# A layer of state-space scan and gated MLP on one core: three projections of a chunk gathered in one phase of full-row matmuls

## The chip, the cores and the metric

The kernel runs on 1 core of one Trainium2 chip. The metric is the time of one execution on the device, in microseconds (us); lower is better. A core has five engines that work side by side, each through its own queue in order: TensorE (PE: matrix products, with its weight loads shown as PEld), VectorE (DVE), ScalarE (ACT), GpSimd (POOL) and SyncE (SP), which here issues transfers (DMAs). Data lie in SBUF, sums of matrix products in PSUM banks.

## What is computed

The input x has 2048 rows of 448 values, in bfloat16. The rows are normalised; the result feeds a state-space recurrence (part A) and a gated MLP (part B), and both are multiplied and added to the input:

```python
def _A_ref(x, Lambda_re, Lambda_im, B_re, B_im, C_re, C_im, log_dt, Dskip):
    dt = jnp.exp(log_dt)
    Lam_bar = jnp.exp(dt * Lam)
    B_bar = ((Lam_bar - 1.0) / Lam)[:, None] * Bmat
    Bu = jnp.einsum("bld,pd->blp", x + 0j, B_bar)
    for t in range(L):
        h = Lam_bar[None, :] * h + Bu[:, t, :]
    y = 2.0 * jnp.einsum("blp,dp->bld", hseq, Cmat).real + x * Dskip[None, None, :]
def _B_ref(x, w_gate, w_up, w_down):      # w_gate, w_up: 448 x 1792; w_down: 1792 x 448
    h = _sigmoid(x @ w_gate) * (x @ w_up)
    return h @ w_down
xn = _layernorm(x)
return x + _A_ref(xn, ...) * silu(_B_ref(xn, ...))
```

## The kernel before, in words

The 2048 rows are cut into four chunks (c = 0 to 3) of 512. `xnT` holds a chunk's normalised rows transposed. Per chunk there are these kinds of work:

- **Gate and up steps** (`gu_step`, `gu_mm` at L709 and L710): 14 steps a chunk, seven blocks `m` for each of gate and up. Each step is seven pairs of matmuls with 64 contraction rows; the two of a pair run at the same time in the two halves of the array. A step fills one of three PSUM slots `gu` (two banks each). `gu_evac` reads it out: a gate step by ScalarE (L723, tanh), an up step by VectorE (L726, times the up values, into `hF`). In chunk 0 the seven gate steps come first, then the seven up steps; in the others they alternate.
- **Input projections of the scan** (`b_units`): four units `pt` a chunk, the products with the input matrix `bT`. Units 0 to 2 have 512 columns in each of two banks; unit 3 is narrow, 256 columns in each, with its weights in `bT6`. The 448 values of a row are three times 128 and one rest of 64. So each unit has a pair of 64-row matmuls (L762 and L763, for unit 3 L765 and L767) and six 128-row ones (L777, for unit 3 L780). ScalarE copies the sums to `bus` (L788; for unit 3 three copies, L792, L794, L796).
- **The scan** (`ssm_pair`, `ssm_stack`, called by `whole`): VectorE products with sine and cosine tables, two scans along the rows, two products more, and the state sequence `hT`. POOL prepares the coefficients, ScalarE and VectorE the tables (`tables`, L577 to L602).
- **Down** (`down`, L892): 14 full-row matmuls for each of four 128-row blocks `j`, into one of two PSUM banks `acc`, then ScalarE's silu (L898, `g_t`).
- **Skip products** (`yout`, L917): seven full-row matmuls from `hT` into `acc`, then three VectorE operations (L923, L925, L927: add, multiply, add) and the store.

Down of chunk c - 1 and the skip products of chunk c - 2 run while chunk c is in its gate and up steps. In each chunk there are two places where full-row work stands between 64-row steps: `b_units(c, (0, 1), ...)` and `b_units(c, (2, 3), ...)`. In each, the 64-row pairs of two units go first, with `start=True`, then a down (the `mid` argument), then the units' full-row matmuls, then a skip product, a down and a skip product (chunks 2 and 3). Between the two places stand three gate and up steps.

The order of PE's queue is that of the calls. For the other engines a planner (`Plan`) decides: each piece of work is registered with an assumed cost, what it reads and what it writes, and the planner places pieces by the latest time at which PE's fixed order needs them. So a change of PE's order also moves work on VectorE, ScalarE and POOL. `SW` is the cost that the planner assumes for a change between 64-row and full-row matmuls. Each engine then works strictly in that order.

Of the kernel before, what the change touches and what calls it, by code (L numbers as in the profile page):

```python
# [14 lines left out]
ACT = mybir.ActivationFunctionType  # L15
# [5 lines left out]
P = 128  # L21
# [41 lines left out]
def act(n, ap=0):  # L63
    return 0.05 + 0.000833 * n + 0.093 * ap
# [9 lines left out]
class Plan:  # L74
# [10 lines left out]
    def add(self, eng, cost, fn, r=(), w=(), dma=0, lat=None, chain=False, name="", rate=230e3):  # L85
        o = Op()
        o.idx, o.eng, o.cost, o.fn, o.dma, o.name = len(self.ops), eng, cost, fn, dma, name
        o.lat = LAT.get(eng, 0.0) if lat is None else lat
        o.pre, o.suc, o.rate = {}, [], rate
        o.slot = None  # L90
        if dma and eng != "POOL":
            o.slot, self.n_dma = self.n_dma, self.n_dma + 1
        o.start = o.end = None
        for k in r:
            if k in self.w:
                self._edge(self.w[k], o, True)
        for k in w:
            for q in self.r.get(k, ()):
                self._edge(q, o, False)
            if k in self.w:  # L100
                self._edge(self.w[k], o, True)
        for k in w:
            self.w[k] = o
            self.r[k] = []
        for k in r:
            if k not in w:
                self.r.setdefault(k, []).append(o)
        if chain or eng == "PE" or (eng == "DVE" and self.seq):
            key = ("chain", eng)
            if key in self.last_of:  # L110
                self._edge(self.last_of[key], o, None)
            self.last_of[key] = o
        self.ops.append(o)
        return o
# [131 lines left out]
def kernel(  # L246
# [274 lines left out]
    def xr(c, lo=0, hi=TPC):  # L521
        return [("xnT", c % 3, j, h) for j in range(lo, hi) for h in "ab"]
# [171 lines left out]
    def next_gu():  # L694
        a = gu_n[0] % 3
        gu_n[0] += 1
        return a
# [51 lines left out]

    bus_n = [0]  # L750

    def b_units(c, pts, mid=None):
        x = xnT[c % 3]
        slots = [next_gu() for _ in pts]
        bk = [("bT", 0), ("bT", 1), ("bT3", 0), ("bT3", 1), "bT3l"] + (
            [("bT6", 0), ("bT6", 1)] + [("bT6", i, h) for i in range(2) for h in range(2)] if 3 in pts else [])

        def pairs():
            for pt, a in zip(pts, slots):
                if pt < 3:  # L760
                    ps = slice(pt * P, pt * P + P)
                    T.matmul(gu[a][:, 0, :], lhsT=bT[0:H, 3, 0, ps], rhs=x[0:H, 6, :], start=True, stop=False)  # L762
                    T.matmul(gu[a][:, 1, :], lhsT=bT[H:P, 3, 1, ps], rhs=x[H:P, 5, :], start=True, stop=False)  # L763
                else:
                    T.matmul(gu[a][:, 0, 0:256], lhsT=bT6[0:H, 3, :], rhs=x[0:H, 6, 0:256],  # L765
                             start=True, stop=False)
                    T.matmul(gu[a][:, 1, 0:256], lhsT=bT6[H:P, 3, :], rhs=x[H:P, 5, 256:512],  # L767
                             start=True, stop=False)
        add("PE", 0.216 * len(pts), pairs, r=xr(c) + bk, w=[("gu", a) for a in slots], name=f"bp{c}.{pts[0]}")
        if mid:  # L770
            mid()
        for n, (pt, a) in enumerate(zip(pts, slots)):
            def fulls(pt=pt, a=a):
                for i in range(2):
                    for kt in range(3):
                        if pt < 3:
                            T.matmul(gu[a][:, i, :], lhsT=bT[:, kt, i, pt * P:pt * P + P], rhs=x[:, 2 * kt, :],  # L777
                                     start=False, stop=(kt == 2))
                        else:
                            T.matmul(gu[a][:, i, 0:256], lhsT=bT6[:, kt, :],  # L780
                                     rhs=x[:, 2 * kt, i * 256:i * 256 + 256], start=False, stop=(kt == 2))
            add("PE", (6 * 0.215 if pt < 3 else 6 * 0.11) + (0 if n or mid else SW), fulls,
                r=xr(c) + bk + [("gu", a)], w=[("gu", a)], name=f"b{c}.{pt}")
            u = bus_n[0] % NBUS
            bus_n[0] += 1
            bus_of[c, pt] = u
            if pt < 3:
                add("ACT", act(1024), lambda u=u, a=a: A.copy(out=bus[u][:], in_=gu[a][:]),  # L788
                    r=[("gu", a)], w=[("bus", u)])
            else:  # L790
                h2 = lambda t: t.rearrange("p (i n) -> p i n", i=2)
                add("ACT", act(512), lambda u=u, a=a: A.copy(out=h2(bus[u][:, 0, :]), in_=gu[a][:, :, 0:256]),  # L792
                    r=[("gu", a)], w=[("bus", u)])
                add("ACT", 0.6, lambda u=u, a=a: A.copy(out=h2(bus[u][0:H, 1, :]), in_=gu[a][H:P, :, 0:256]),  # L794
                    r=[("gu", a)], w=[("bus", u, 1)])
                add("ACT", 0.6, lambda u=u, a=a: A.copy(out=h2(bus[u][H:P, 1, :]), in_=gu[a][0:H, :, 0:256]),  # L796
                    r=[("gu", a)], w=[("bus", u, 2)])

    bus_of = {}

# [50 lines left out]
    def ssm_stack(c):  # L851
        pt = 3
        u = bus_of[c, pt]
        ia, ta = nxt("ta")
        iz, z = nxt("z")
        iw, wv = nxt("wv")
        tk = [("cos", 3), ("sin", 3)]
        dve(dve2(1024), lambda: V.tensor_tensor(out=ta[:], in0=bus[u][:], in1=cs3[:], op=ALU.mult),
            [("bus", u), ("bus", u, 1), ("bus", u, 2)] + tk, [("ta", ia)])
        dve(dve2(512), lambda: V.tensor_tensor(out=z[:, 0, :], in0=ta[:, 0, :], in1=ta[:, 1, :], op=ALU.add),  # L860
            [("ta", ia)], [("z", iz)])
        rb = C("r")[:, pt:pt + 1].to_broadcast((P, L))
        dve(1.194, lambda: V.tensor_tensor_scan(out=wv[:, 0, :], data0=rb, data1=z[:, 0, :],
                                                initial=(st[pt][:, 0, :] if c else 0.0), op0=ALU.mult, op1=ALU.add),
            ["r", ("z", iz)] + ([("st", pt)] if c else []), [("wv", iw)])
        for h in range(2):
            o, i = slice(h * H, h * H + H), slice((1 - h) * H, (1 - h) * H + H)
            add("ACT", 0.6, lambda o=o, i=i: A.copy(out=wv[o, 1, :], in_=wv[i, 0, :]), r=[("wv", iw)], w=[("wv", iw, 1 + h)])
        wk = [("wv", iw), ("wv", iw, 1), ("wv", iw, 2)]
        if c < NC_ - 1:  # L870
            dve(0.12, lambda: V.tensor_tensor(out=tqs[pt][:, 0, :], in0=wv[:, 1, L - 1:L], in1=sinL[:, 3, 0, :], op=ALU.mult),
                wk + ["sinL"], [("tq", pt)])
            dve(0.12, lambda: V.scalar_tensor_tensor(out=st[pt][:, 0, :], in0=wv[:, 0, L - 1:L], scalar=cosL[:, pt, :],
                                                    in1=tqs[pt][:, 0, :], op0=ALU.mult, op1=ALU.subtract),
                wk + ["cosL", ("tq", pt)], [("st", pt)])
        ia, tcx = nxt("ta")
        dve(dve2(1024), lambda: V.tensor_tensor(out=tcx[:], in0=wv[:], in1=cs3[:], op=ALU.mult), wk + tk, [("ta", ia)])
        dve(dve2(512), lambda: V.tensor_tensor(out=hT[c % 2][:, 6, :], in0=tcx[:, 0, :], in1=tcx[:, 1, :], op=ALU.subtract),
            [("ta", ia)], hkeys(c, pt))
# [113 lines left out]
        gu_step(0, i)  # L993
    stats_for(2)
    stats_for(3)
    b_units(0, (0, 1))
    b_units(0, (2, 3))
    for i in range(13, 14):
        gu_step(0, i, i == 13)
    c_scale()  # L1000
    whole(0)

    halves(1, ((0, "g"), (1, "g")))
    one(1, 0, "u")
    prepare(2)
    b_units(1, (0, 1), lambda: down(0, 0, True))
    down(0, 1)
    for i in range(3, 6):
        gu_step(1, i, i == 3)
    b_units(1, (2, 3), lambda: down(0, 2, True))  # L1010
    down(0, 3)
    for i in range(6, 14):
        gu_step(1, i, i == 6)
    whole(1)
    for c in (2, 3):
        for i in range(0, 4):
            gu_step(c, i)
        b_units(c, (0, 1), lambda: down(c - 1, 0, True))
        yout(c - 2, 0)
        down(c - 1, 1)  # L1020
        yout(c - 2, 1)
        for i in range(4, 7):
            gu_step(c, i, i == 4)
        b_units(c, (2, 3), lambda: down(c - 1, 2, True))
        yout(c - 2, 2)
        down(c - 1, 3)
        yout(c - 2, 3)
        if c == 2:
            prepare(3)
        for i in range(7, 14):  # L1030
            gu_step(c, i, i == 7)
        whole(c)

    yout(2, 0, True)
# [53 lines left out]
```

## Time and profile before

| | us |
|---|---|
| median of 4 runs | 187.07 (186.75 to 188.67) |
| the profiled execution | 186.84 |
| its span, first to last instruction | 185.0 |
| VectorE busy | 165.9 |
| ScalarE busy | 93.0 |

The span is the time from the first instruction to the last in the profile; the execution's own time is 1.84 us longer. Busy time of an engine is the union of its instructions. In a timeline each row gives start, duration, engine, source line, operation, tiles written and read with their shapes, the number of merged instructions, and in brackets the idle time before it with what released it. Matmuls are pipelined, so their durations overlap: what counts is the distance from one start to the next. In a row by windows, the width of the window comes first, then busy time (and number of instructions) of PE, PEld, DVE, ACT and POOL, then the granted clock of TensorE, and the DMAs' share and rate.

Two rows of the costliest groups give the scale; after the bar stand busy time in us and the mean ns of one:

```profile
L892 PE MATMUL acc<-wd,hF 128*128 128x448 bf16 x168 | 33.8, 353 | 0.0
L777 PE MATMUL gu<-xnT,bT 128*128 128x512 bf16 x72 | 16.9, 379 | 0.0
```

### The profile page before, as it was taken

To read this page: it belongs to the slowest core of one execution; us is meant where nothing else is said; L and a number is where in the kernel's file an instruction comes from. 1 tells how busy PE (TensorE), PEld (TensorE's weight loads), DVE (VectorE), ACT (ScalarE), POOL (GpSimd) and SP (SyncE) were. 2 spreads that over 40 slices of the span, in tenths; PEclk is the share of its full clock that TensorE was granted. 3 is DMA by queue.
4 is the path that set the end of the run, shared out by engine and by line. 5 is a ranking of instruction groups with operands and counts; after the bars stand their busy time and mean duration, and the time that the engine had idled before them with its cause. 6 is when DMAs were issued, how large, how long until landed. Compare 5 with 4: busy or idle time off the path is not lost.

```text
span 185.0 us, 3527 instructions
## 1 busy us (share of the span) xinstructions
PE 179.3 (97%) x1375; PEld 88.2 (48%) x1375; DVE 165.9 (90%) x295; ACT 93.0 (50%) x140; POOL 38.4 (21%) x93
## 2 busy tenths in 40 slices
PE   7999999999999999999999999999999999999991
PEld 2684443564445444444445444444445544455550
DVE  3833999999999899999999999899999999999763
ACT  3549996973999994225465432327124526211110
POOL 7134452930268926000012100000000000000000
PEclk9999999999999999999999999999999999999999
DMA  5999999499202330000023200000000000002120
GB/s 135 275 217 233 220 217 136 81 265 208 88 4 50 78 74 0 0 0 4 0 57 84 61 26 0 4 25 25 0 25 4 25 25 4 25 0 76 51 78 25
DMA packets 30257, 13.43 MB, mean 73 GB/s; under 512 B 19744, under 2 KB 30240, under 8 KB 30240
## 3 DMA queue, kind: packets, MB, share of 16 engines
q1 hardware_dynamic: 28336, 12.05, 30.3%
q10 hardware_dynamic: 1808, 1.15, 2.4%
q8 instruction: 11, 0.18, 0.4%
q14 instruction: 6, 0.05, 0.1%
q0 software_dynamic: 96, 0.00, 0.0%
HBM read 6.77 MB, written 1.84 MB: 47 GB/s over the span
## 4 chain that ended last, share of the span: by engine, by line
PE 80%; DVE 11%; ACT 4%; issue 1%; DMA 1%; DVEq 0%
PE gu L709 39%; PE acc L892 15%; PE acc L917 11%; PE gu L892 6%; PE gu L777 5%; DVE hF L726 2%; DVE wv L831 2%; DMA x_all<-in_A_x_dram 1%; ACT ctmp L675 1%; DVE ta L824 1%; PE gu L780 1%; PE acc L502 1%; ACT bus L788 1%; DVE tb L825 1%; PE gu L710 1%
## 5 line engine op out<-in xcount | busy, mean ns | idle before, releaser
L709 PE MATMUL gu<-xnT,wG 64*128 64x512 bf16 (+1 forms) x231 | 46.1, 344 | 0.3 <-DVE xnT L510 0.3
L710 PE MATMUL gu<-xnT,wG 64*128 64x512 bf16 (+1 forms) x231 | 46.1, 344 | 0.0
L709 PE MATMUL gu<-xnT,wU 64*128 64x512 bf16 x196 | 46.0, 376 | 0.0
L710 PE MATMUL gu<-xnT,wU 64*128 64x512 bf16 x196 | 46.0, 376 | 0.0
L723 ACT ACTIVATE sig<-gu 128x1024 f32<-128x1024 f32 x21 | 21.4, 1022 | 30.3 <-PE gu L710 27.9
L892 PE MATMUL acc<-wd,hF 128*128 128x448 bf16 x168 | 33.8, 353 | 0.0
L892 PEld LDWEIGHTS <-hF 128*128 128x128 bf16 x224 | 21.4, 98 | 21.1 <-issue 1.7
L709 PEld LDWEIGHTS <-wG 64*128 64x128 bf16 x231 | 21.3, 94 | 20.9 <-issue 1.9
L709 PEld LDWEIGHTS <-wU 64*128 64x128 bf16 x196 | 18.1, 94 | 23.4 <-issue 1.3
L726 DVE SCALAR_TENSOR_TENSOR hF<-sig,gu 128x1024 bf16<-128x1024 f32 x21 | 25.4, 1211 | 1.9 <-PE gu L710 1.6
L831 DVE TENSOR_TENSOR_SCAN wv<-c_r,st,z 128x512 bf16<-128x512 f32 x18 | 22.9, 1274 | 0.0
L917 PE MATMUL acc<-cT,hT 128*128 128x448 bf16 (+1 forms) x112 | 22.4, 344 | 0.0
L710 PEld LDWEIGHTS <-wG 64*128 64x128 bf16 x231 | 21.3, 94 | 0.0
L710 PEld LDWEIGHTS <-wU 64*128 64x128 bf16 x196 | 18.1, 94 | 0.0
L777 PE MATMUL gu<-xnT,bT 128*128 128x512 bf16 x72 | 16.9, 379 | 0.0
L917 PEld LDWEIGHTS <-hT 128*128 128x128 bf16 x119 | 11.3, 98 | 10.0 <-issue 0.4
L898 ACT ACTIVATE g_t<-acc 128x448 bf16<-128x448 f32 x12 | 6.5, 540 | 16.1 <-PE acc L892 13.0
L425 DVE BATCH_NORM_STATS2 bst<-x_all 128x6 f32<-128x448 bf16 x12 | 7.0, 611 | 7.1 <-DMA x_all<-in_A_x_dram 7.1
L788 ACT CAST bus<-gu 128x1024 bf16<-128x1024 f32 x12 | 12.0, 1005 | 2.3 <-PE gu L777 2.3
L478 POOL COPY xn<-xn 128x64 bf16<-128x64 bf16 x12 | 5.8, 481 | 29.3 <-ACT xn L475 29.1
L923 DVE TENSOR_TENSOR o_t<-acc,xd 128x448 bf16<-128x448 f32 (+1 forms) x16 | 9.5, 594 | 2.6 <-PE acc L917 2.4
L898 ACT ACTIVATE g_t<-gu 128x448 bf16<-128x448 f32 x4 | 2.2, 544 | 18.8 <-PE gu L892 18.8
(142 smaller groups left out, 260.5 us busy)
## 6 DMA issues: line engine op xcount, KB each, us to landing
out_dram<-o_t SPq DMA_DIRECT2D x15, 112.0 KB, 1.7
wd<-in_B_w_down_dram SPq DMA_DIRECT2D x2, 784.0 KB, 5.0
x_all<-in_A_x_dram SPq DMA_DIRECT2D x3, 448.0 KB, 5.0
wU<-in_B_w_up_dram SPq DMA_DIRECT2D x2, 448.0 KB, 11.1
wU<-in_B_w_up_dram SPq DMA_DIRECT2D x2, 336.0 KB, 7.2
wG<-in_B_w_gate_dram SPq DMA_DIRECT2D x2, 224.0 KB, 5.7
wG<-in_B_w_gate_dram ACTq DMA_DIRECT2D x2, 224.0 KB, 6.4
xnT<-xn SPq DMA_TRANSPOSE x24, 2.4
```

What stands on the lines that cost most here:

```text
L425: add("DVE", 0.6, lambda: V.bn_stats(out=bst[b][:], in_=x_all[:, t, :]), r=[("x", t)], w=[("bst", b)])
L709: T.matmul(gu[a][:, 0, ts], lhsT=w_[0:H, s, ms], rhs=x[0:H, s, ts], start=(s == 0), stop=(s == 6))
L710: T.matmul(gu[a][:, 1, ts], lhsT=w_[H:P, (s + 1) % 7, ms], rhs=x[H:P, s, ts], start=(s == 0), stop=(s == 6))
L723: add("ACT", act(1024), lambda: A.activation(th, gu[a][:], ACT.Tanh, scale=0.5), r=[("gu", a)], w=[tk])
L726: add("DVE", dve1(1024), lambda: V.scalar_tensor_tensor(out=ho, in0=th, scalar=1.0, in1=gu[a][:], op0=ALU.add, op1=ALU.mult), r=[("gu", a) ...
L777: T.matmul(gu[a][:, i, :], lhsT=bT[:, kt, i, pt * P:pt * P + P], rhs=x[:, 2 * kt, :], start=False, stop=(kt == 2))
L788: add("ACT", act(1024), lambda u=u, a=a: A.copy(out=bus[u][:], in_=gu[a][:]), r=[("gu", a)], w=[("bus", u)])
L831: dve(1.194, lambda k=k: V.tensor_tensor_scan(out=wv[:, k, :], data0=rb, data1=z[:, k, :], initial=(st[pt][:, k, :] if c else 0.0), op0=AL ...
L892: T.matmul(d, lhsT=hF[c % 2][:, m, h, js], rhs=wd[:, ft, :], start=(ft == 0), stop=(ft == FT - 1))
L898: add("ACT", act(448), lambda: A.activation(g_t[g][:], d, ACT.Silu, scale=0.5), r=[key, "silutab"], w=[("gt", g)])
L917: T.matmul(y, lhsT=hT[c % 2][:, hm, js], rhs=cT[:, cm, c0:c1], start=(i == 0), stop=(i == 6))
L923: add("DVE", dve1(n), lambda od=od, y=y, c0=c0, c1=c1: V.tensor_tensor(out=od, in0=y, in1=xq[:, c0:c1], op=ALU.add), r=[key, ("xd", q)], w ...
```

## The change

There is one full-row phase a chunk in place of two. `b_phase` puts the 64-row pairs of units 3, 0 and 1 first, then their full-row matmuls, then (`mid`) all four downs of chunk c - 1 with the four skip products of chunk c - 2 between them, then unit 2: its full-row matmuls open the sum and its 64-row pair closes it, directly ahead of the next 64-row step. Unit 3 moves from a `gu` slot into the two `acc` banks, 256 columns in each, and its sums are copied by six ScalarE instructions of 256 columns in place of three of 512. Chunk 0's last up step now stands ahead of the phase. The number and the sizes of the matmuls stay the same.

```diff
-    def b_units(c, pts, mid=None):
+    def b_phase(c, mid=None):
         x = xnT[c % 3]
-        slots = [next_gu() for _ in pts]
...
+        slots = [next_gu() for _ in range(3)]
+        a3 = (next_acc(), next_acc())
...
+        rs = [(slice(0, H), 6), (slice(H, P), 5)]
+
+        def halfrows(pt, start):
+            for i, (hs, s_) in enumerate(rs):
+                if pt < 3:
+                    T.matmul(gu[slots[pt]][:, i, :], lhsT=bT[hs, 3, i, pt * P:pt * P + P], rhs=x[hs, s_, :],
+                             start=start, stop=not start)
+                else:
+                    T.matmul(acc[a3[i]][:, 0:256], lhsT=bT6[hs, 3, :], rhs=x[hs, s_, i * 256:i * 256 + 256],
+                             start=start, stop=not start)
 
         def pairs():
...
+            for pt in (3, 0, 1):
+                halfrows(pt, True)
+
+        def fulls(pt, first):
+            for i in range(2):
+                for kt in range(3):
+                    if pt < 3:
+                        T.matmul(gu[slots[pt]][:, i, :], lhsT=bT[:, kt, i, pt * P:pt * P + P], rhs=x[:, 2 * kt, :],
+                                 start=(first and kt == 0), stop=(not first and kt == 2))
+                    else:
+                        T.matmul(acc[a3[i]][:, 0:256], lhsT=bT6[:, kt, :],
+                                 rhs=x[:, 2 * kt, i * 256:i * 256 + 256], start=False, stop=(kt == 2))
...
+            if pt < 3:
+                add("ACT", act(1024), lambda: A.copy(out=bus[u][:], in_=gu[slots[pt]][:]), r=key(pt), w=[("bus", u)])
+                return
+            for i in range(2):
+                ns = slice(i * 256, i * 256 + 256)
+                for h, (d, q, l) in enumerate(((slice(0, P), slice(0, P), 0), (slice(0, H), slice(H, P), 1),
+                                               (slice(H, P), slice(0, H), 1))):
+                    add("ACT", 0.3, lambda ns=ns, d=d, q=q, l=l, i=i: A.copy(out=bus[u][d, l, ns], in_=acc[a3[i]][q, 0:256]),
...
+        add("PE", 0.54, pairs, r=xr(c) + bk + bk6, w=key(3) + key(0) + key(1), name=f"bp{c}")
+        for pt in (3, 0, 1):
+            add("PE", (1.29 if pt < 3 else 0.66) + (SW if pt == 3 else 0), lambda pt=pt: fulls(pt, False),
+                r=xr(c) + bk + bk6 + key(pt), w=key(pt), name=f"b{c}.{pt}")
+            evac(pt)
+        if mid:
+            mid()
+        add("PE", 1.29, lambda: fulls(2, True), r=xr(c) + bk, w=key(2), name=f"b{c}.2")
+        add("PE", 0.22 + SW, lambda: halfrows(2, False), r=xr(c) + bk + key(2), w=key(2), name=f"bp{c}.2")
+        evac(2)
...
-    b_units(0, (0, 1))
-    b_units(0, (2, 3))
-    for i in range(13, 14):
-        gu_step(0, i, i == 13)
+    gu_step(0, 13)
+    b_phase(0)
...
-    b_units(1, (0, 1), lambda: down(0, 0, True))
-    down(0, 1)
-    for i in range(3, 6):
-        gu_step(1, i, i == 3)
-    b_units(1, (2, 3), lambda: down(0, 2, True))
-    down(0, 3)
-    for i in range(6, 14):
-        gu_step(1, i, i == 6)
+    b_phase(1, lambda: [down(0, j) for j in range(4)])
+    for i in range(3, 14):
+        gu_step(1, i)
     whole(1)
     for c in (2, 3):
+        def mid(c=c):
+            for j in range(4):
+                down(c - 1, j)
+                yout(c - 2, j)
         for i in range(0, 4):
             gu_step(c, i)
...
+        b_phase(c, mid)
         if c == 2:
             prepare(3)
-        for i in range(7, 14):
-            gu_step(c, i, i == 7)
+        for i in range(4, 14):
+            gu_step(c, i)
         whole(c)
```

More of the change, by code (lines that the diff above doesn't have):

```diff
@@ L750 @@
     bus_n = [0]
-    def b_units(c, pts, mid=None):
+    def b_phase(c, mid=None):
         x = xnT[c % 3]
-        slots = [next_gu() for _ in pts]
-        bk = [("bT", 0), ("bT", 1), ("bT3", 0), ("bT3", 1), "bT3l"] + (
-            [("bT6", 0), ("bT6", 1)] + [("bT6", i, h) for i in range(2) for h in range(2)] if 3 in pts else [])
-        def pairs():
[L759 to L783, printed above, removed]
@@ new lines, in b_phase @@
+        slots = [next_gu() for _ in range(3)]
+        a3 = (next_acc(), next_acc())
+        bk = [("bT", 0), ("bT", 1), ("bT3", 0), ("bT3", 1), "bT3l"]
+        bk6 = [("bT6", 0), ("bT6", 1)] + [("bT6", i, h) for i in range(2) for h in range(2)]
+        rs = [(slice(0, H), 6), (slice(H, P), 5)]
[7 more added lines that the diff above has]
+                             start=start, stop=not start)
@@ L784, in b_units, with key, evac @@
+        def key(pt):
+            return [("gu", slots[pt])] if pt < 3 else [("acc", a) for a in a3]
+        def evac(pt):
             u = bus_n[0] % NBUS
@@ L787, in b_units @@
             if pt < 3:
[L788 to L797, printed above, removed]
+                add("ACT", act(1024), lambda: A.copy(out=bus[u][:], in_=gu[slots[pt]][:]), r=key(pt), w=[("bus", u)])
[5 more added lines that the diff above has]
+                    add("ACT", 0.3, lambda ns=ns, d=d, q=q, l=l, i=i: A.copy(out=bus[u][d, l, ns], in_=acc[a3[i]][q, 0:256]),
+                        r=[("acc", a3[i])] + ([("bus", u, i, 0)] if h else []),
+                        w=[("bus", u) if h == i == 0 else ("bus", u, i, h)])
+        add("PE", 0.54, pairs, r=xr(c) + bk + bk6, w=key(3) + key(0) + key(1), name=f"bp{c}")
[8 more added lines that the diff above has]
+        evac(2)
     bus_of = {}
@@ L858, in ssm_stack @@
         dve(dve2(1024), lambda: V.tensor_tensor(out=ta[:], in0=bus[u][:], in1=cs3[:], op=ALU.mult),
-            [("bus", u), ("bus", u, 1), ("bus", u, 2)] + tk, [("ta", ia)])
+            [("bus", u)] + [("bus", u, i, h) for i in range(2) for h in range(3) if i or h] + tk, [("ta", ia)])
         dve(dve2(512), lambda: V.tensor_tensor(out=z[:, 0, :], in0=ta[:, 0, :], in1=ta[:, 1, :], op=ALU.add),
@@ L1005 @@
     prepare(2)
-    b_units(1, (0, 1), lambda: down(0, 0, True))
-    down(0, 1)
-    for i in range(3, 6):
-        gu_step(1, i, i == 3)
-    b_units(1, (2, 3), lambda: down(0, 2, True))
-    down(0, 3)
-    for i in range(6, 14):
-        gu_step(1, i, i == 6)
+    b_phase(1, lambda: [down(0, j) for j in range(4)])
+    for i in range(3, 14):
+        gu_step(1, i)
     whole(1)
     for c in (2, 3):
+        def mid(c=c):
+            for j in range(4):
+                down(c - 1, j)
+                yout(c - 2, j)
         for i in range(0, 4):
             gu_step(c, i)
[L1018 to L1027, printed above, removed]
+        b_phase(c, mid)
         if c == 2:
             prepare(3)
-        for i in range(7, 14):
-            gu_step(c, i, i == 7)
+        for i in range(4, 14):
+            gu_step(c, i)
         whole(c)
```

## Prediction

> **What bounds the kernel now.** I read the busy totals first, then the chain that ended last.
>
> ```profile
> PE 179.3 (97%) x1375; PEld 88.2 (48%) x1375; DVE 165.9 (90%) x295; ACT 93.0 (50%) x140; POOL 38.4 (21%) x93
> ...
> PE 80%; DVE 11%; ACT 4%; issue 1%; DMA 1%; DVEq 0%
> ```
>
> TensorE (PE) is busy for all of the span but its first microseconds, so whatever shortens its queue shortens the kernel, and any new wait lengthens it. VectorE is close behind. The busy time by windows says how close:
>
> ```profile
> 60.00:110.00 50.00, 50.00 (x373) 23.50 (x372) 49.28 (x81) 26.08 (x40) 11.39 (x19) 1.00 0.17 36
> ```
>
> In these 50 us PE never stops (first number after the width), VectorE (third pair) has 0.7 us idle, and ScalarE (fourth) is half idle. The clock is 1.00. So the questions are what PE's queue loses, and whether VectorE, in its new order, still serves PE in time.
>
> **A crossing between half rows and full rows.** The PE timeline around chunk 1's first phase (L762: 64-row pairs, L892 and L777: 128-row matmuls, L709: 64-row again):
>
> ```profile
> 40.75 0.38 PE L762 MATMUL gu<-xnT,bT 64*128 64x512 bf16 x1
> ...
> 40.96 0.38 PE L762 MATMUL gu<-xnT,bT 64*128 64x512 bf16 x1
> ...
> 41.27 2.82 PE L892 MATMUL acc<-wd,hF 128*128 128x448 bf16 x14
> 43.93 2.75 PE L777 MATMUL gu<-xnT,bT 128*128 128x512 bf16 x12
> 46.52 2.81 PE L892 MATMUL acc<-wd,hF 128*128 128x448 bf16 x14
> 49.27 0.39 PE L709 MATMUL gu<-xnT,wU 64*128 64x512 bf16 x1
> ```
>
> A 512-column pair takes 0.21 start to start (40.75 to 40.96), but the one ahead of the full rows takes 0.31: 0.10 for going in. The down block that stays in full rows takes 2.66 (41.27 to 43.93), the one that goes back to half rows 2.75 (46.52 to 49.27): 0.09 for going out, and 0.01 more in the step behind it. The old kernel crosses four times a chunk, the built queue of the new one twice, over four chunks: 8 crossings fewer. At 0.10 that is -0.80 us; between 0.09 and 0.11, -0.72 to -0.88. The matmuls are as many and as large as before (1375 of each kind), so nothing else leaves the queue. I use 0.10, which these rows measure directly.
>
> A rule says otherwise. The Trainium skill's "TensorEngine Tiling (Array Packing)", Key Properties, has every change of tiling mode drain the array, and "TensorE: Matmul & The Clock Gate", Single matmul latency, gives a matmul alone 398 cycles at 2.4 GHz beside its columns, 0.166 us. If a crossing laid all of that open, the estimate would be 8 x 0.166 = 1.3 us saved instead of 0.80; the rows show less, and decide.
>
> **A wait that goes.** PE and ScalarE in chunk 1's second phase:
>
> ```profile
> 53.22 1.00 ACT L723 ACTIVATE sig<-gu 128x1024 f32<-128x1024 f32 x1
> ...
> 53.81 0.38 PE L762 MATMUL gu<-xnT,bT 64*128 64x512 bf16 x1
> ...
> 54.28 0.27 PE L765 MATMUL gu<-xnT,bT 64*128 64x256 bf16 x1
> ```
>
> Unit 3's pair follows after 0.47, in chunk 2 after 0.22 (95.70 to 95.92): it waited 0.25 for its PSUM slot, whose gate step ScalarE was still reading until 54.22; 0.06 later PE went on. ScalarE was late because two L432 statistics stood ahead. In the new kernel this pair writes the acc banks, idle there. The next such place is unit 1's pair in chunk 1, laid out at 41.2; ScalarE's back-to-back reads of the two gate steps before it end near 40.8 (ends of 38.6 and 39.4, 0.24 behind, 0.9 each). So -0.25, or 0 if another read is late.
>
> **A wait that comes.** The new order moves three VectorE operations of the sine tables, one L579 and two L581, ahead of all of chunk 0's up products (L726). Before:
>
> ```profile
> 22.00 2.40 DVE L726 SCALAR_TENSOR_TENSOR hF<-hF,gu 128x1024 bf16<-128x1024 bf16 x2
> ...
> 25.87 0.42 DVE L579 TENSOR_SCALAR hT<-hT 128x513 f32<-128x513 f32 x1
> 26.21 1.21 DVE L726 SCALAR_TENSOR_TENSOR hF<-hF,gu 128x1024 bf16<-128x1024 bf16 x1
> 27.64 1.22 DVE L726 SCALAR_TENSOR_TENSOR hF<-hF,gu 128x1024 bf16<-128x1024 bf16 x1 [0.22 <-PE gu L710]
> 28.78 1.29 DVE L581 SCALAR_TENSOR_TENSOR hT<-hT,hT 128x513 f32<-128x513 f32 x2
> 29.98 1.21 DVE L726 SCALAR_TENSOR_TENSOR hF<-hF,gu 128x1024 bf16<-128x1024 bf16 x1
> ```
>
> The first up product ends at 23.22 and frees the slot that the fourth up step needs; PE starts that step at 24.41:
>
> ```profile
> 24.41 0.38 PE L709 MATMUL gu<-xnT,wU 64*128 64x512 bf16 x1
> ```
>
> With 0.06 for the release, VectorE had 1.13 to spare. Moved ahead of it: 0.34 (25.87 to 26.21) and 1.20 (28.78 to 29.98), 1.54. So PE waits 1.54 - 1.13 = +0.41. Nothing is idle there to absorb it, and PE never regains it. The next ones catch up: VectorE takes 1.14 a product, PE 1.51 a step. Bounds: 0, if the x rows that VectorE waited 5 us for at 16.8 land 0.4 earlier; 1.54, if it has no slack left.
>
> **What lies beside other work.** Unit 3's three ScalarE copies of 512 become six of 256. From 1.00 for 1024 and 0.59 for 512 (L788, L792), a straight line gives 0.38 for 256: 6 x 0.38 - 3 x 0.58 = +0.5 a chunk, 2.1 us in all on an engine busy 93 of 185. They hold the acc banks that the downs want next: units 0 and 1 (2 x 1.29 us of matmul) stand between, three copies take 1.14. Cost nothing; uncovered, up to 0.5 a chunk. "TensorEngine Tiling (Array Packing)", PSUM Bottleneck, advises reading several tiles of a bank in one instruction, the opposite of this edit; were PSUM reading the limit, the estimate would be +2.1 us. ScalarE's idle half says no.
>
> POOL's first coefficient product (L611) now stands ahead of the last three bT6 copies and waits for ScalarE's c_cth, near 26.6 (25.1 for the xn rows, 1.2 for L584, 0.3 for L602); the copies then end near 27.8, and PE wants them near 30.9. SP's DMAs keep their order. The four downs with their skip products now run as one block (4 x 2.65 + 4 x 1.32 = 15.9 us in chunks 2 and 3) without an up step, so VectorE's products stand in longer stretches of state-space work. Laying its new queue end to end with the steps of its rows (0.60 for a 1024 product, 1.20 for a scan, 1.14 for an up product, 0.30 and 0.58 for output rows), the tightest late places hold. Chunk 2: the third skip product ends on PE at 95.4; its add at 95.6 (0.58), 8.1 of state-space rows, then the third up product (1.2) end at 105.5; PE wants the slot after a down (2.65), a skip product (1.32), unit 2 with its crossing and pair (1.61) and four steps (6.04), at 107.1: 1.5 to spare. End: the last hT write of chunk 3 at 170.0, the product that reads it at 172.0: 2.0 to spare, where the old trace has 169.2 and 172.8.
>
> **Sum.** -0.80 - 0.25 + 0.41 = -0.64. The profiled run took 186.84 (span 185.0, 1.84 around it), 0.23 below the median of 187.07. So 186.2 for that run, and 186.4 for the median.
>
> **Rivals.** A, no new wait: the table work fits (DMA earlier), 187.07 - 1.05 = 186.0. For it, the place is paced by a landing; against, all moved rows are measured. B, the wait is larger, up to 1.54, or ScalarE's moved copies keep the 0.25: 187.07 - 0.80 + 1.54 = 187.8. C, slower: VectorE becomes the bound. Its place is the first skip product of chunk 3, which needs the last hT write. VectorE idles where unit copies or up steps come late (the layout has 1.1 us near 58.7 that the old trace lacks), and at 98% busy it never wins that back. It decides beyond 2.0 us of further lateness; 5 us late means +3.0, 189.4. For it speaks the window row, against it the layout. That the crossings are not saved at all is no rival: the built queue shows two a chunk.
>
> **Numbers.** Forecast 0.60, A 0.15, B 0.12, C 0.13. Low end: -0.88 - 0.25 + 0 gives 185.9; high end: B's 187.8 and the near part of C, 188.1. A measurement of this kernel tells about 1% from no change (runs from 186.75 to 188.67), so faster means below 185.2 and slower above 188.9. Nothing in the sum reaches 185.2: 0.04. Most of C and a little of B's tail lie above: 0.12. Within: 0.84.
>
> **What would show it.** Two crossings a chunk, each 0.09 to 0.11 beyond the beat; no wait at unit 3's pair; a wait of about 0.4 ahead of the fourth up step near 24.4, released by VectorE; PE without idle after that, and 2 us between the last hT write and its reader. Wrong if PE waits elsewhere: for L726 behind state-space rows, for the acc banks, or for hT at the end.

## The result, and the profile after

The changed kernel takes 186.73 us (median of 54 runs, 185.81 to 188.11), the kernel before 187.29 in the same comparison (78 runs). The ratio is 0.9972, 95% interval 0.9962 to 0.9982: a real gain of some 0.5 us, well inside the 1% band. The profiled execution of the changed kernel took 186.49 with a span of 184.6, 0.35 less than the one of before. Ratios here and below leave out the executions in a slower state of the chip, of which the last run of the table below had one; the medians are of all.

In the changed kernel's lines the down is L905 with its silu at L911, the skip product L930 with L936, L938 and L940, and the copies of the sums are L791 and, for unit 3, L797.

Busy totals and the chain that ended last:

```profile
PE 178.6 (97%) x1375; PEld 89.2 (48%) x1375; DVE 166.3 (90%) x295; ACT 95.0 (51%) x152; POOL 34.4 (19%) x93
...
PE 96%; DVE 2%; issue 0%; DVEq 0%
```

Where the old chain went over VectorE for 11%, now 96% of it is TensorE's own queue. The same 50 us by windows:

```profile
60.00:110.00 50.00, 50.00 (x386) 23.68 (x382) 48.13 (x75) 26.61 (x43) 9.89 (x20) 1.00 0.16 36
```

PE still never stops, but VectorE (third pair) is busy for 48.13 instead of 49.28: it now stands idle 1.15 us longer here. Its longest waits here are two for an up step of PE, of 0.60 and 0.59, and one of 0.34 for a skip product; before, it had one of 0.62 for a ScalarE copy.

```profile
74.16 1.22 DVE L726 SCALAR_TENSOR_TENSOR hF<-sig,gu 128x1024 bf16<-128x1024 f32 x1 [0.60 <-PE gu L710]
...
107.65 1.22 DVE L726 SCALAR_TENSOR_TENSOR hF<-sig,gu 128x1024 bf16<-128x1024 f32 x1 [0.59 <-PE gu L710]
```

From 110 to 160 it is the other way round: VectorE is busy for 48.94, before for 48.48. That returns below.

PE's timeline, chunk 2's phase first, then the fourth up step of chunk 0:

```profile
80.03 0.59 PE L763 MATMUL gu<-xnT,bT 64*128 64x512 bf16 x4
80.56 0.83 PE L780 MATMUL acc<-xnT,bT 128*128 128x256 bf16 x6
...
99.71 1.46 PE L777 MATMUL gu<-xnT,bT 128*128 128x512 bf16 x6
101.10 0.39 PE L763 MATMUL gu<-xnT,bT 64*128 64x512 bf16 x2
...
24.16 0.38 PE L709 MATMUL gu<-xnT,wU 64*128 64x512 bf16 x1
...
25.03 0.37 PE L709 MATMUL gu<-xnT,wU 64*128 64x512 bf16 x1 [0.49 <-DVE hF L726]
```

The last two pairs of 64 rows take 0.53 (80.03 to 80.56): twice the beat of 0.21 and 0.10 for going into full rows. Unit 2's six matmuls take 1.39 (99.71 to 101.10), six beats of 0.213 and 0.11 for coming back. Nineteen microseconds lie between, and nothing crosses in them. The fourth up step starts 0.87 after the matmul before it instead of 0.21: a wait of 0.66 for VectorE's first up product.

What VectorE did ahead of that product:

```profile
17.13 0.63 DVE L425 BATCH_NORM_STATS2 bst<-x_all 128x6 f32<-128x448 bf16 x1 [5.34 <-DMA x_all<-in_A_x_dram]
...
22.22 0.42 DVE L579 TENSOR_SCALAR hT<-hT 128x513 f32<-128x513 f32 x1
22.56 1.29 DVE L581 SCALAR_TENSOR_TENSOR hT<-hT,hT 128x513 f32<-128x513 f32 x2
23.76 4.61 DVE L726 SCALAR_TENSOR_TENSOR hF<-hF,gu 128x1024 bf16<-128x1024 bf16 x4
```

The table work stands where the prediction put it, and before everything come 5.34 us of waiting for the x rows, which in this execution landed 0.32 later than in the one of before (16.81).

PE's last matmul ends 0.39 earlier than before. The distances from start to start, summed over the whole trace, account for it: crossings -0.78, the wait at unit 3's pair in chunk 1 gone, -0.26, the wait at the fourth up step +0.66, and small differences of +0.02 and -0.03.

### The profile page after: what moved, and what is told of

Same layout as the page of the kernel before. It is cut to its first block, busy times and chain, and to the rows that moved or that the text cites. A ratio compares the mean times of both kernels' runs of the same rounds, so it can differ in the third digit from the quotient of the medians.

```text
span 184.6 us, 3546 instructions
## 1 busy us (share of the span) xinstructions
PE 178.6 (97%) x1375; PEld 89.2 (48%) x1375; DVE 166.3 (90%) x295; ACT 95.0 (51%) x152; POOL 34.4 (19%) x93
## 3 DMA queue, kind: packets, MB, share of 16 engines
q10 hardware_dynamic: 1808, 1.15, 2.4%
## 4 chain that ended last, share of the span: by engine, by line
PE 96%; DVE 2%; issue 0%; DVEq 0%
PE gu L709 44%; PE acc L905 17%; PE acc L930 11%; PE gu L777 8%; PE gu L905 6%; PE gu L419 2%; PE acc L780 2%; PE gu L763 2%; PE gu L710 1%; PE acc L502 1%; DVE hF L726 1%; PE gu L930 1%; PE acc L503 0%; DVE hT L581 0%; DVE xnT L510 0%
## 5 line engine op out<-in xcount | busy, mean ns | idle before, releaser
L905 PE MATMUL acc<-wd,hF 128*128 128x448 bf16 x168 | 33.3, 352 | 0.0
L905 PEld LDWEIGHTS <-hF 128*128 128x128 bf16 x224 | 21.9, 98 | 20.7 <-issue 0.2
L709 PEld LDWEIGHTS <-wU 64*128 64x128 bf16 x196 | 18.4, 94 | 22.3
L930 PE MATMUL acc<-cT,hT 128*128 128x448 bf16 (+1 forms) x112 | 22.4, 344 | 0.0
L791 ACT CAST bus<-gu 128x1024 bf16<-128x1024 f32 x12 | 11.9, 1012 | 14.0 <-PE gu L763 13.2
L710 PEld LDWEIGHTS <-wU 64*128 64x128 bf16 x196 | 18.3, 94 | 0.8 <-issue 0.8
L930 PEld LDWEIGHTS <-hT 128*128 128x128 bf16 x119 | 11.3, 98 | 10.2 <-issue 0.4
L911 ACT ACTIVATE g_t<-acc 128x448 bf16<-128x448 f32 x12 | 6.5, 538 | 13.1 <-PE acc L905 12.8
L911 ACT ACTIVATE g_t<-gu 128x448 bf16<-128x448 f32 x4 | 2.2, 543 | 18.9 <-PE gu L905 12.4
L797 ACT CAST bus<-acc 64x256 bf16<-64x256 f32 (+1 forms) x24 | 8.7, 368 | 5.5 <-PE acc L780 5.2
L905 PE MATMUL gu<-wd,hF 128*128 128x448 bf16 x56 | 11.2, 352 | 0.0
```

What stands on the lines that cost most here:

```text
L709: T.matmul(gu[a][:, 0, ts], lhsT=w_[0:H, s, ms], rhs=x[0:H, s, ts], start=(s == 0), stop=(s == 6))
L710: T.matmul(gu[a][:, 1, ts], lhsT=w_[H:P, (s + 1) % 7, ms], rhs=x[H:P, s, ts], start=(s == 0), stop=(s == 6))
L791: add("ACT", act(1024), lambda: A.copy(out=bus[u][:], in_=gu[slots[pt]][:]), r=key(pt), w=[("bus", u)])
L797: add("ACT", 0.3, lambda ns=ns, d=d, q=q, l=l, i=i: A.copy(out=bus[u][d, l, ns], in_=acc[a3[i]][q, 0:256]), r=[("acc", a3[i])] + ([("bus", ...
L905: T.matmul(d, lhsT=hF[c % 2][:, m, h, js], rhs=wd[:, ft, :], start=(ft == 0), stop=(ft == FT - 1))
L911: add("ACT", act(448), lambda: A.activation(g_t[g][:], d, ACT.Silu, scale=0.5), r=[key, "silutab"], w=[("gt", g)])
```

## The experiments

Ratios are to the kernel before, measured on the same chip; medians in us. The runs stand on three chips, on which the kernel before took 187.54 (the first four rows), 187.34 and 187.14, so that a difference of two medians can hold 0.2 to 0.4 of the chips.

| run | median | ratio (95% interval) |
|---|---|---|
| tables late | 186.83 | 0.9961 (0.9941 to 0.9982) |
| before, tables early | 188.69 | 1.0051 (1.0028 to 1.0073) |
| eight crossings back | 187.56 | 1.0022 (0.9993 to 1.0051) |
| before, statistics late | 187.30 | 0.9989 (0.9964 to 1.0014) |
| rows first | 186.02 | 0.9922 (0.9894 to 0.9949) |
| rows first, tables late | 186.28 | 0.9941 (0.9918 to 0.9964) |
| copies twice | 191.29 | 1.0235 (1.0184 to 1.0286) |
| six products more | 190.95 | 1.0193 (1.0161 to 1.0226) |
| before, rows first | 187.37 | 1.0018 (0.9999 to 1.0036) |
| rows first, eight crossings back | 186.74 | 0.9977 (0.9963 to 0.9991) |
| two products more | 188.19 | 1.0058 (1.0038 to 1.0079) |
| before, two products more | 187.80 | 1.0022 (0.9990 to 1.0055) |

**Tables late.** The changed kernel, with the planner told that the table operations may come later (`bias` is added to their due time).

```diff
-                r=[vk], w=[nk])
+                r=[vk], w=[nk], bias=(6.0 if pt == 3 else 0.0))
...
-                r=[vk, nk], w=[nk])
+                r=[vk, nk], w=[nk], bias=(6.0 if pt >= 2 else 0.0))
```

> The changed kernel with one thing undone: the last sine-table operations on VectorE (one L579, two L581) stand between chunk 0's up products again instead of ahead of them; PE's order is the changed one. Theory: the wait ahead of the fourth up step (0.66 us in the changed kernel's profile) is gone and all of it comes off the end: 0.4 to 0.7 us below the changed kernel, about 186.1, ratio to the kernel before 0.993 to 0.995. Rival (the wait is made up later, by slack further down PE's queue): 186.7, ratio 0.997.

The wait at the fourth up step is gone, yet the time is that of the changed kernel. In its VectorE and PE timelines:

```profile
17.29 0.63 DVE L425 BATCH_NORM_STATS2 bst<-x_all 128x6 f32<-128x448 bf16 x1 [5.14 <-DMA x_all<-in_A_x_dram]
...
31.48 0.39 PE L763 MATMUL gu<-xnT,bT 64*128 64x512 bf16 x2 [0.21 <-DVE hF L726]
```

PE now waits 0.38 at unit 1's pair, seven microseconds later, for VectorE's sixth up product, which has the same table work ahead of it. The wait was moved more than removed. Two causes remain: the table work itself, or the rows that came late (17.29) ahead of all of it.

**Before, tables early.** The kernel before, with every table operation ahead of chunk 0's first up product.

```diff
-                r=[("gu", a), tk], w=[hk])
+                r=[("gu", a), tk] + [("nu", p) for p in range(4) if c == 0], w=[hk])
```

> The kernel before with that one part of the change alone: all table operations of VectorE ahead of chunk 0's first up product, PE's order as before. Theory: a wait of 0.3 to 0.7 us ahead of the fourth up step, released by VectorE, and 0.3 to 0.7 us more at the end: about 187.8, ratio 1.002 to 1.004. Rival (VectorE's order there is free): ratio 1.000.

It is slower by half a per cent, and PE waits 0.91 at the fourth up step. But the planner also moved later VectorE work, and most of the loss is elsewhere, at unit 3's pair in chunk 2; the view of waits has both:

```profile
PE gu L765 <- DVE hF L726: 1.0, 1, 1.0
PE gu L709 <- DVE hF L726: 0.7, 1, 0.7
```

So the run shows that the move alone makes a wait at this step, and does not give its price.

**Eight crossings back.** The changed kernel, with unit 1's 64-row pair between unit 0's full rows and its own; the other engines' orders stay.

```diff
-            for pt in (3, 0, 1):
+            for pt in (3, 0):
                 halfrows(pt, True)
...
-            for i in range(2):
+            for i in ([halfrows(1, True)] if pt == 1 else [0]) and range(2):
```

> The changed kernel with unit 1's 64-row pair put between the full-row matmuls of unit 0 and its own: two crossings more in each chunk, eight in all, the same matmuls, and every other engine's order untouched. Theory: eight times 0.09 to 0.11 us, +0.8 us on the changed kernel, about 187.5, ratio 1.000 to 1.002; each new crossing 0.31 from start to start where a 512-column pair or matmul takes 0.215. Rival (a crossing is hidden and the gain came from the fewer phases in another way): ratio 0.997.

0.8 us over the changed kernel by the medians, 0.9 by the ratios with an interval of 0.6 to either side; over all crossings of the trace the time beyond the beat rises from 1.80 to 2.63, 0.83 for eight. The profiled execution also has a wait of 1.30 at the fourth up step, twice that of the changed kernel, though nothing ahead of that step was edited: the x rows landed at 17.62.

**Before, statistics late.** The kernel before, with chunk 3's row statistics (L432) behind the gate step that they had delayed.

```diff
-                r=[("x", t), "silutab"], w=[("sm", t), "junk"])
+                r=[("x", t), "silutab", ("sig", 0)], w=[("sm", t), "junk"])
...
-    stats_for(3)
...
         gu_step(1, i, i == 3)
+    stats_for(3)
```

> The kernel before, with ScalarE's two row statistics (L432) of chunk 3 moved behind the gate step that unit 3's pair of chunk 1 waits for. Theory: that pair follows 0.22 after unit 2's instead of 0.47, and 0.25 us come off the end: about 187.0, ratio 0.9982 to 0.9992. Rival (the wait only moves to a later place): ratio 1.000.

The wait at unit 3's pair in chunk 1 is gone, which supports its cause, and a wait of 0.37 for an up product at chunk 2's unit 3 has come, since VectorE's order changed with it. The time, 0.9989, tells neither from nothing.

**Rows first, with the tables early and late.** The x rows 4 to 7 are asked for ahead of the first up weights; only SyncE's order changes.

```diff
     def emit(self):
+        q = sorted((o for o in self.ops if o.eng == "SP" and o.dma), key=lambda o: o.start); q[6].start = q[4].start - 1e-6
```

> The changed kernel with one SyncE transfer moved: the x rows 4 to 7 are asked for ahead of the first two up-weight transfers (672 KB) instead of behind them. The orders on TensorE, VectorE, ScalarE and GpSimd are those of the changed kernel, the table work still ahead of the first up product. Theory (the wait ahead of the fourth up step, 0.66 us in the changed kernel's trace, is paced by the landing of these rows: VectorE stood idle 5.34 us for them until 17.13): 672 KB at the 190 to 230 GB/s of those slices bring the rows 2.9 to 3.5 us forward, VectorE's first statistics start near 14, its first up product starts as soon as the first up step is done (before 22.6 instead of 23.76), the wait at the fourth up step is gone, and no new wait comes at unit 1's pair, since the table work is done in time that was idle. About 186.1 us against the changed kernel's 186.7, ratio to the kernel before .993 to .995. Rival (the place of the table work decides, and something other than the rows paces it, ScalarE's sines or the statistics' way over GpSimd): the wait stays, ratio .997. Second rival: the up weights come too late and TensorE waits ahead of the first up step at 19.84.

> The run with the table work between the up products again, and with the x rows asked for first as in the run above. Theory (in that run the wait had only moved to unit 1's pair at 31.48, because the same VectorE work lies ahead of it there): earlier rows do not help where the table work stands behind up products that wait for TensorE, so 0.2 to 0.4 us of wait stay at unit 1's pair, and the time is that of the run with the tables late, ratio .995 to .997, some 0.3 us above the run with the rows first alone. Rival (all that matters is when the rows land): both runs with the rows first are equal, ratio .993 to .995, with no wait in either.

The first of the two is the fastest kernel of this study, 186.02, below the kernel before and the changed one. Its VectorE timeline:

```profile
14.37 0.63 DVE L425 BATCH_NORM_STATS2 bst<-x_all 128x6 f32<-128x448 bf16 x1 [2.13 <-DMA x_all<-in_A_x_dram]
...
22.25 2.56 DVE L726 SCALAR_TENSOR_TENSOR hF<-hF,gu 128x1024 bf16<-128x1024 bf16 x2
```

The rows land 2.8 earlier, the first up product starts 1.5 earlier, and PE waits at none of chunk 0's up steps. But the fourth up step starts at 24.83, only 0.20 ahead of the changed kernel's, because PE itself got there later: in this execution its first gate step waited for gate weights.

```profile
7.94 0.28 PE L710 MATMUL gu<-xnT,wG 64*128 64x256 bf16 x1 [0.48 <-DMA wG<-in_B_w_gate_dram]
```

The profiled executions are 0.32 apart, the medians 0.71. In the second run PE does not wait at unit 1's pair either, against what I expected: 186.28, and the intervals of the two overlap. So the wait of the tables-late kernel, too, was the rows' landing, and where the tables stand decides little once the rows are early.

That explains how the wait varies. Here are all profiled executions with the changed kernel's VectorE order ahead of this step and the rows' old place in SyncE's queue (us from the start of the span; the rows' landing is taken where VectorE's first statistics of them start; "there" is when PE would have begun the step):

| execution of | rows land | first up product starts | PE there | wait |
|---|---|---|---|---|
| changed kernel | 17.13 | 23.76 | 24.37 | 0.66 |
| eight crossings back | 17.62 | 24.26 | 24.23 | 1.30 |
| copies twice | 17.08 | 23.71 | 24.76 | 0.22 |
| six products more | 17.60 | 24.23 | 25.08 | 0.41 |
| two products more | 16.81 | 23.44 | 24.38 | 0.33 |

The product starts 6.63 after the rows land, each time; in the kernel before it was 5.19 (16.81 to 22.00), and 1.44 is the moved work. PE gets there 16.9 after chunk 0's first gate step starts, and in all five executions that start, between 7.33 and 8.19, follows by 0.15 the end of a VectorE copy of the first transposed rows (`xnT`, L510); the gate weights had landed by then. The changed kernel's waits name it:

```profile
PE gu L709 <- DVE xnT L510: 0.3, 1, 0.3
```

So the wait is a race between the landing of the rows 4 to 7 and the way of the first rows to that copy. In the mean of the five the step starts at 25.15, in the two executions with the rows first and the tables early (24.83, and 24.71 in a run below) at 24.77. That is 0.4 of the 0.7 between the medians; the rest is not explained.

**Before, rows first.** The same one line in the kernel before.

> The kernel before with the x rows 4 to 7 asked for ahead of the first two up-weight transfers, orders on the four compute engines untouched. It takes the landing of these rows out of the comparison with the changed kernel in the same form, 186.02 us, ratio .9922. Theory (the change in itself is worth 0.80 for eight crossings and 0.25 for the wait at unit 3's pair in chunk 1, and the rest of it was given back to the rows' landing; in the kernel before the rows are in time in most executions, 1.13 us to spare in the profiled one): ratio .998 to 1.000, about 187.1, so that the change measures about 1.05 us between the two. Rival (early rows help any order alike): ratio .994 to .996 here too, and the change is worth 0.5 as before.

No gain: 1.0018. Early rows help only the order that waits for them. With the landing out of the comparison the change takes 0.9922 against 1.0018, 1.8 us with an interval of 0.6 to either side, or 1.35 by the medians, which stand on two chips; I had expected 1.05. The profiled execution of this run shows 0.56 of wait at unit 3's pair in chunk 1, where the one of before had 0.26, ScalarE's gate read starting at 53.78 instead of 53.22; with 0.80 for the crossings that makes 1.36; the two profiled executions are 1.28 apart. Why ScalarE is later there was not tried.

**Rows first, eight crossings back.** The two edits together, so that no landing blurs the price.

> The changed kernel with the x rows first and with unit 1's 64-row pair put back between unit 0's and its own full rows: two crossings more a chunk, eight in all, nothing else moved, and no landing wait to blur it (in the run with the crossings alone that wait was 1.30 us). Theory: eight crossings at 0.09 to 0.11 give 0.7 to 0.9 us over the run with the rows first, 186.8, ratio .996 to .997. Rival (a crossing costs the 0.166 us of a matmul's whole latency): 1.3 us, 187.3, ratio .999.

186.74 against 186.02: 0.72 for eight, 0.09 each, by the medians on two chips; by the ratios 1.0, with an interval of 0.6 to either side. The trace is sharper: summed over all crossings 2.59 against 1.76, 0.10 each. The row of chunk 2, out of full rows and in again behind one pair:

```profile
82.50 0.39 PE L763 MATMUL gu<-xnT,bT 64*128 64x512 bf16 x2
82.82 1.04 PE L777 MATMUL gu<-xnT,bT 128*128 128x512 bf16 x4
```

0.32 for a pair whose beat is 0.21.

**Copies twice.** The changed kernel with each of unit 3's six ScalarE copies issued twice.

```diff
-... lambda ns=ns, d=d, q=q, l=l, i=i: A.copy(out=bus[u][d, l, ns], in_=acc[a3[i]][q, 0:256]),
+... lambda ns=ns, d=d, q=q, l=l, i=i: [A.copy(out=bus[u][d, l, ns], in_=acc[a3[i]][q, 0:256]) for _ in range(2)],
```

> The changed kernel with each of unit 3's six ScalarE copies per chunk issued twice: 24 copies more at 0.37 us, 8.7 us more ScalarE work, 2.2 us a chunk; the second copy writes the same values. Orders on the other engines are unchanged. Theory (the copies are hidden, ScalarE is half idle): the time stays within 0.3 us of the changed kernel, ratio .996 to 1.000, with ScalarE's busy time near 104 instead of 95. Rival (ScalarE's copies stand on the way to unit 0's and unit 1's buses and to the next gates, so that their cost was part of the change's): 0.5 us or more a chunk reaches TensorE, +2 us, ratio about 1.007, with TensorE waiting at a step released by ScalarE.

My theory fell: 4.6 us over the changed kernel for 8.2 us more of ScalarE's busy time, on an engine that is at 54%. PE waits 1.07, 0.78, 0.91, 0.45 and 1.72 at five places, four of them downs that want an `acc` bank. Chunk 3's phase on ScalarE and PE in the changed kernel:

```profile
123.65 2.28 ACT L797 CAST bus<-acc 128x256 bf16<-128x256 f32 x6 [1.46 <-PE acc L780]
125.96 1.24 ACT L881 COPY wv<-wv 64x512 bf16<-64x512 bf16 x2
127.22 1.93 ACT L791 CAST bus<-gu 128x1024 bf16<-128x1024 f32 x2
129.22 0.54 ACT L911 ACTIVATE g_t<-acc 128x448 bf16<-128x448 f32 x1
...
130.34 0.92 PE L905 MATMUL acc<-wd,hF 128*128 128x448 bf16 x4
```

and with the copies twice:

```profile
126.88 4.68 ACT L797 CAST bus<-acc 128x256 bf16<-128x256 f32 x12 [1.46 <-PE acc L780]
...
134.67 0.56 ACT L911 ACTIVATE g_t<-acc 128x448 bf16<-128x448 f32 x1
135.29 2.81 PE L905 MATMUL acc<-wd,hF 128*128 128x448 bf16 x14 [1.55 <-ACT g_t L911]
```

ScalarE works without a gap from unit 3's first copy to the silu that empties a down's bank. In the changed kernel PE's down gives way to its next block at 129.02, the silu starts at 129.22, 0.07 after ScalarE's last copy, and ends at 129.76, 0.58 ahead of the next down that wants the bank. So beyond the copies that stand there this phase has 0.65 us to spare, not half an engine. The run agrees: its copies take 2.40 longer (4.68 against 2.28) and PE waits 1.72 for that bank, so 0.68 was covered.

**Six and two products more in the tail.** VectorE's product at L858 of chunk 3's unit 2 repeated, in the changed kernel six times and twice, in the kernel before twice (the same line there is L845).

```diff
-... lambda: V.tensor_tensor(out=tcx[:], in0=wv[:], in1=cosb, op=ALU.mult), wk + tk, [("ta", ia)])
+... lambda: [V.tensor_tensor(out=tcx[:], in0=wv[:], in1=cosb, op=ALU.mult) for _ in range(7 if (c, pt) == (3, 2) else 1)], wk + tk, [("ta", ia)])
```

> The changed kernel with one of VectorE's products of the last chunk's unit 2 (line 858, 0.6 us) repeated six times more: 3.6 us more VectorE work ahead of the last hT write; the repeats write the same values. Theory (the prediction's margin: that last write at 170.0 against its reader at 172.0, 2.0 us to spare; in the changed kernel the last down and output steps follow it): 3.6 less 2.0 gives about 1.6 us more, 188.3 against 186.7, ratio 1.005, with TensorE waiting for VectorE's hT ahead of the last output step. Rival 1 (more slack than counted): no change, ratio .997. Rival 2 (no slack): all 3.6 us, ratio 1.016.

All of it comes through: the repeats took 4.37 (0.73 each), and PE waits 2.78 at the first of the last output steps and 1.57 at the third, 4.34 in all. So the margin of 2.0 was read at the wrong place. VectorE at the end of the kernel before, its output add of L923 being that of L936 in the changed kernel:

```profile
172.46 0.69 DVE L483 TENSOR_TENSOR xd<-xn,dbc 128x448 bf16<-128x448 bf16 x2
174.35 0.62 DVE L923 TENSOR_TENSOR o_t<-acc,xd 128x448 bf16<-128x448 f32 x1 [1.20 <-PE acc L917]
```

and of the changed kernel, with PE's row of the three output steps:

```profile
172.43 4.13 PE L930 MATMUL acc<-cT,hT 128*128 128x448 bf16 x21
...
173.78 0.69 DVE L483 TENSOR_TENSOR xd<-xn,dbc 128x448 bf16<-128x448 bf16 x2
174.38 0.61 DVE L936 TENSOR_TENSOR o_t<-acc,xd 128x448 bf16<-128x448 f32 x1
```

The three steps share two banks. The third starts 2.65 after the first, at 175.08, and wants the bank that the add at 174.38 leaves at 174.99: 0.09 to spare, and 0.03 with the 0.06 for a release taken off, which is also the difference between 4.37 and 4.34. In the kernel before VectorE had first 1.20 of idle time, then 0.51 to the third step at 175.47: 1.71. The next two runs test this.

> The changed kernel with the same product of chunk 3's unit 2 repeated twice more: by the run with six repeats, which took 0.73 us each, 1.46 us of VectorE work. Theory (VectorE's spare in the tail is not the 1.6 to 2.0 us at the first of chunk 3's output steps but the 0.09 us at the third, which waits for VectorE to have read the first one's accumulator: read done at 174.99, step begun at 175.08): 1.37 us reach the end, 188.1, ratio 1.003 to 1.006, TensorE waiting at that third step for the output add. Rival (the spare is 1.6 us): no change, ratio .997.

> The kernel before with the same two repeats, 1.46 us of VectorE work. Theory (there VectorE had 1.20 us of idle time ahead of the first output add and 0.51 us after it until the third output step, 1.71 in all, and it is the change that used this up): no change, ratio .998 to 1.002, and no wait of TensorE in the tail. Rival (the tail is as tight in the kernel before): 0.9 to 1.5 us, ratio 1.005 to 1.008.

In the changed kernel 1.46 us of work cost 1.46 by the medians, and PE waits 1.42 at the third output step:

```profile
172.11 2.81 PE L930 MATMUL acc<-cT,hT 128*128 128x448 bf16 x14
176.18 1.48 PE L930 MATMUL acc<-cT,hT 128*128 128x448 bf16 x7 [1.26 <-DVE o_t L936]
```

In the kernel before, PE does not wait in the tail, and its profiled execution takes 186.84 with the work as without it. Its ratio, 1.0022 (0.9990 to 1.0055), goes with that but would not show it alone: the interval reaches to 1.0 us, and the median lies 0.66 above the kernel before on that chip.

## Why the prediction came out right, step by step

- **Crossings, -0.80.** Right: -0.78 in the trace, and 0.83 for eight in the traces of both runs that put them back; the times, 0.7 to 1.0, agree but are less sharp. The estimate from the Trainium skill, 1.3 us by "TensorE: Matmul & The Clock Gate", Single matmul latency, is not what these runs show. "TensorEngine Tiling (Array Packing)", Key Properties, has a change of tiling mode drain the array; the runs agree in so far as each change costs time, 0.10.
- **The wait that goes, -0.25.** Right: -0.26, and the run with the statistics late has it gone as well. In the kernel before its size varies: 0.56 in the run with the rows first.
- **The wait that comes, +0.41.** The right place, engine and cause; the size holds for the landing that it was worked out from. In the execution where the rows landed at 16.81, as in the trace of before, the wait is 0.33, and the moved work took 1.44 where I added up 1.54. In the profiled execution of the changed kernel it is 0.66. I had named the landing as a way to no wait, but not that it goes as far the other way: the bound of 0 belongs to it, and so does 1.30. Rival A, no new wait, is the kernel with the rows first.
- **ScalarE's copies, nothing.** The size is right: the copies take 0.37 each where the line gave 0.38, and PE waits nowhere for them. The reason is wrong. "ScalarE's idle half" is a mean over the kernel, and what counts is the phase itself, which had 0.65 us left beside the longer copies. The estimate of 2.1 us, which stood beside "TensorEngine Tiling (Array Packing)", PSUM Bottleneck, for the case that PSUM reading were the limit, did not appear.
- **POOL, nothing.** Right: L611 starts at 26.73, the `bT6` copies end at 27.80, and PE wants them near 31.
- **VectorE's margins.** Chunk 2's third up product ends at 105.86 and its slot is wanted at 107.37, 1.5 as in the layout. At the end the step failed: it measured the last `hT` write against its reader (170.25 and 172.43, 2.2), and the margin that decides, 0.09, is at the accumulator of the third output step. Rival C's mechanism took place in part: VectorE stood idle 1.15 us longer between 60 and 110 and won 0.46 of it back between 110 and 160. Up to the tail it was idle 0.76 longer in all and busy 0.47 longer, so that it comes there 1.23 later while PE comes 0.39 earlier; together 1.62 of 1.71. Rival C was less than 0.1 us away from adding to the time, and I had given it a distance of 2.0.
- **Sum, -0.64.** The medians show -0.56, inside the range. In the profiled executions it is -0.35, since the wait was 0.66. With the waits that the table of landings has, 0.22 to 1.30, the same terms give anything from -0.82 to +0.26 for one execution, and -0.46 with their mean of 0.58; that the sum of -0.64 lies so near the medians is luck in part. And it is luck that the tail added nothing: the margin read for it was 2.0, and the one that decides was under 0.1.

## What to carry to other kernels

A margin is read where a buffer comes free, not only where data is wanted: walk the last readers of every bank that the bounding engine uses next. A share of busy time says nothing of the cover in one phase; take the row that ends just before the wait, and count to it. And where a step hangs on a transfer, one trace gives one landing: ask first for what is wanted first, and the wait that hung on it goes.

## What was not expected of the hardware

- With the queue's order unchanged, the x rows landed between 16.81 and 17.74 in ten profiled executions of different kernels. Moved ahead of two transfers of 336 KB they landed between 13.20 and 14.97 in four.
- A VectorE product of 1024 columns (L858) took 0.60 from start to start in a stream of different ones. Repeated into the same tile it took 0.73 each. Why was not tried.
- ScalarE's copies of 256 columns out of the `acc` banks took the same time for 64 and for 128 partitions, 0.366 and 0.373 in the mean.
